# A hand-written order of 300 steps, written anew, with two filler matmuls fewer

## The chip, the cores and the metric

The kernel runs on one core of a Trainium2 chip. A core has five engines that run their own instruction queues and wait for each other through semaphores: TensorE (PE; its weight loads are shown apart as PEld), VectorE (DVE), ScalarE (ACT), GpSimd (POOL) and SyncE (SP), which here issues nearly all DMAs. The metric is the device time of one execution in microseconds.

## The reference

The input x (2048 tokens of 448) is normalized over its columns. The output is x plus two branches of the normalized xn: a linear attention and a feed-forward block.

```python
def _A_ref(x, wqkv, w_phi, wo):
    qkv = (x @ wqkv)...                                  # 16 heads of 28
    pq = jnp.einsum("bhsd,hdf->bhsf", q, w_phi)
    pk = jnp.einsum("bhsd,hdf->bhsf", k, w_phi)
    phi_q = concatenate([softmax(pq), softmax(-pq)])
    phi_k = concatenate([softmax(pk), softmax(-pk)])
    kv = einsum("bhsf,bhsd->bhfd", phi_k, v); z = phi_k summed over s
    num = einsum("bhqf,bhfd->bhqd", phi_q, kv)
    den = einsum("bhqf,bhf->bhq", phi_q, z)[..., None] + 1e-6
    return (num / den) @ wo
def _B_ref(x, w1, b1, w2):
    h = x @ w1 + b1                                      # 1792 columns
    return (h * tanh(softplus(h))) @ w2
xn = _layernorm(x)
return x + _A_ref(xn, ...) + _B_ref(xn, ...)
```

## The kernel before

Tokens are taken in 16 tiles t of 128, two tiles to a unit u. Everything is written as small named steps, and one string, `ORDER`, lists the roughly 300 steps in the order in which they are recorded (`run_order`). Recording a step appends its instructions to the queues of the engines that it uses, so this one list sets the order on every engine at once; `Program.resolve` then adds the semaphore waits that the data need. PSUM banks are handed out in the order of recording too: `take2` gives the pair of banks that was used longest ago, so a step waits for whatever last read those banks. Engines run in order: an instruction that waits holds up all behind it on its queue, and on SP it holds up every later DMA.

The names. `lx..`, `lkm`, `lkt`, `lvm`, `l1..`, `l2`, `lo`, `lb` load x, the k weights (three chunks of 128 rows, then the tail of 64 rows twice), v's, W1 (three chunks `l1m0` to `l1m2` and tails `l1t`), W2, Wo and the bias; `lqT0` to `lqT3` load wqkv's q columns with a DMA transpose (L285). `z18` is 18 filler matmuls on a constant (L376), which nobody reads. `st6d` is the statistics of tile 6 on VectorE (`a`: on ScalarE), `rs`/`xn` the normalization of a unit (L464 to L492; `p`: on POOL, `d`: on VectorE), and `xt` the transposition of xn into xnT, where contraction runs over partitions: by TensorE and copies (`b`, `a`, `d`; L500), or by one DMA transpose from SP (`m`; L512). `wtk` transposes the k weights on TensorE (L552) and `wmk`, `wmq` multiply phi into the k and q weights (L576), so that pk and pq come from xn directly.

`k2F` and `k2H` are the two parts of unit 2's matmuls for k, `q2F` and `q2H` for q, `v2F` and `v2H` for v, all of them at L430: the contraction of 448 is three whole chunks of 128 rows (F, six matmuls for the two tiles) and a half chunk of 64 rows (H, two matmuls on two halves of the array). F and H may stand in either order, with other steps between; after the second, ScalarE or VectorE empties the two banks: for k and q with two exps each (L614, L675), for v with a copy (L505 or L507). `e3` is the DMA transpose of tile 3's exps of q (L683), again from SP. `kn2.0` sums exps of k per head on VectorE (L622, L624) and scales them on POOL (L626). `f1.2F`/`f1.2H` are the two parts of the FFN's first product for the second half of the tokens and chunk 2 of 14 (L430), followed by ScalarE's Mish (L694). `kv0` to `kv7` (L643) sum phi_k with v, `kvz` brings that into a masked form and transposes it by DMA (L661). `nd5` is the numerator and denominator of tile 5 (L717) and its seven VectorE operations (L732 to L743), `ot` the transposition of the result by DMA (L752), `g5` the FFN's second product for tile 5 (L818), `wo2F`/`wo2H` the output projection of unit 2 (L834), then VectorE adds the residual (L783) and `sto` stores. On POOL, `pi` makes the identity matrix that TensorE's transposes read and the small constant in the normalization's root, `pm`, `pk` masks, `pw`, `pp`, `pv` fills, `bd` the block-diagonal phi.

The tiles keep the names of their buffers in the trace: exps of q lie in `actT` or `Eq`, exps of k in `actT`, xn in four buffers, and the transposed attention results take the places of `Wkv`, `WqT` and `Wpk`.

Of the kernel before, what the change touches and what calls it, by code (L numbers as in the profile page):

```python
# [144 lines left out]


ORDER = """
lx3s lx1s lkms lpa lkts lvms lx2s lqT1 lqT2 st6d table z18 pi st7a pp rs3t st2d st3d pw pm pv lqT0 lqT3 lx6s xn3d rs1a
xn1d wtk0b xt3b wtk1b bd xt1b wmk0a st5d v3Ha st4d qd lx0s v3Fa lx4s wmk1a rs2p xn2p v1Fd wmq1d wmq0a k1F st14d k1H
st15d rs7p v1Hd xn7p xt2m q3H q1H st8d st9d st11d st1d q3F rs4p pk xn4d q1F k3F st10d l1m0s k3H rs5p k2H st12d st0d  # L150
rs0p st13d xn5d q2H lbs q2F k2F xt7m e3 rs6p xt4m e2 xn6p e7 v2Fa v7Fa k7F xt5m v2Hd xn0p v7Hd k7H kn7.0 kn2.0 l1m2s
q4H q4F k4F kn1.0 kn2.1 v4Fa v4Ha k4H e4 k5H xt6m v5Ha kn1.1 kn7.1 v5Fa k5F q6F xt0m kn3.0 k6F k6H v6Hd e6 e5 q6H q5H
l1ts v6Fd q5F l1m1s v0Fd e8 k0F kn5.1 b1 kn6.0 k0H kn3.1 kn4.1 v0Ha f1.2H f1.3H e12 e11 f1.2F f1.3F f0.2F e9 f1.5F e10
e13 f0.2H kn5.0 f1.5H q0H q7H kn4.0 kn0.1 kn6.1 q7F ep kn0.0 f1.0F f0.5F q0F f0.1F f0.1H f1.0H f0.5H kv3 kv1 kv6 kv2
kv4 e15 e0 kv5 kv7 kv0 e14 f0.8H f1.8H f0.8F kvz f0.13F f1.8F f0.7F f0.13H nd3 f1.6H f0.7H e1 f1.6F f0.12F nd1 f0.12H
nd2 f0.3H f0.3F ot1m l2s los f0.11F f0.6F f0.6H f0.11H nd6 f1.1H f1.1F f0.10F f1.11H nd7 f0.9H f0.10H ot3m f0.9F
f1.11F f1.12F f0.4H nd11 f1.9H f0.4F f1.9F f1.4F f1.4H f0.0H f1.12H nd0 ot0m wob f0.0F f1.10F f1.7F f1.13H nd10 f1.7H
f1.10H f1.13F g1 nd4 nd5 ot2m ot5m nd12 wo0H g0 wo1F g3 wo0F g10 nd13 wo1H wo5H nd14 g11 wo5F sto0 ot6m g2 g4 nd15 nd9
wo2H nd8 g5 g13 g14 wo3F ot7m wo7F wo2F g7 g9 g6 g12 wo7H wo3H ot4m sto1 stt14 wo6H wo4H wo4F sto3 wo6F g8 sto5 sto2
sto4 g15 sto6 stt15  # L160
"""


# [806 lines left out]
```

## Time and profile before

| | us |
|---|---|
| median of 3 runs (153.37 to 154.47) | 154.28 |
| the profiled execution | 153.66 |
| its span on the core | 151.8 |
| TensorE busy in the span | 148.0 |

The granted TensorE clock is 1.00. In the views of the profile times count from the start of the span. A row of the timeline gives start, busy time, engine, line, operation and shape, and `xN` where N instructions of one line were merged; in brackets stands how long the engine sat idle before it and what released it. "SPq" rows are DMA issues on SP: their time is that of the issue, not of the transfer. The rows of DMA issues give the size and the median time from issue to landing. Matmuls are pipelined and their ends are modelled, so that their starts are compared, not their busy times.

### The profile page before, as it was taken

The page shows a single profiled execution, that of the slowest core. Times are in us where ns is not written, and L with a number is a line of the kernel's source. Part 1 is how long each engine was busy: PE and PEld are TensorE (multiplying, and loading weights), DVE is VectorE, ACT ScalarE, POOL GpSimd, SP SyncE. Part 2 cuts the span into 40 slices and gives each one's busy share as a digit, 9 for nine tenths or more (in the row PEclk, how much of TensorE's full clock was granted, in tenths as well). Part 3 has the DMA queues.
Part 4 walks back from the last instruction along what each step waited for, and adds up shares of the span by engine and source line. Part 5 has one row for each costly group of instructions (what it writes and reads, how often), then busy time and mean ns, then how long its engine had stood idle before and what let it go on. Part 6 is the DMA issues. An engine that isn't in the chain of part 4 may idle for free.

```text
span 151.8 us, 2910 instructions
## 1 busy us (share of the span) xinstructions
PE 148.0 (97%) x1187; PEld 73.1 (48%) x1187; DVE 100.1 (66%) x224; ACT 72.5 (48%) x87; POOL 45.0 (30%) x66
## 2 busy tenths in 40 slices
PE   7999999999999999999999999999999999999993
PEld 2565454444344466444444444555554655554452
DVE  0977997998799603079986477597896894300631
ACT  3886997897898997585664767000000000000000
POOL 7315888999999960000000000000000000000000
DMA  4997789999996095700099703005230031300234
GB/s 136 294 135 292 181 153 182 223 211 151 224 235 126 0 107 109 138 0 0 15 225 347 173 4 60 0 4 107 77 60 0 4 60 32 89 4 0 95 117 151
DMA packets 39994, 17.17 MB, mean 113 GB/s; under 512 B 33965, under 2 KB 39213, under 8 KB 39981
## 3 DMA queue, kind: packets, MB, share of 16 engines
q1 hardware_dynamic: 39372, 16.87, 50.6%
q8 instruction: 9, 0.15, 0.4%
q10 hardware_dynamic: 608, 0.12, 0.4%
q14 instruction: 5, 0.03, 0.1%
HBM read 7.02 MB, written 1.84 MB: 58 GB/s over the span
## 4 chain that ended last, share of the span: by engine, by line
PE 92%; DMA 2%; SPq 2%; DVE 1%; issue 0%
PE PS L430 46%; PE PS L818 28%; PE PS L834 7%; PE PS L376 4%; PE PS L717 3%; DMA xnT<-xn 2%; PE PS L643 2%; PE PS L576 1%; SPq L683 1%; DVE v_all L507 1%; PE PS L500 1%; PE PS L552 1%; SPq L277 1%; DVE x_all L783 0%; SPq L512 0%
## 5 line engine op out<-in xcount | busy, mean ns | idle before, releaser
L430 PE MATMUL PS<-xnT,W 128*128 128x512 bf16 (+1 forms) x224 | 46.0, 380 | 0.3 <-issue 0.3
L818 PE MATMUL PS<-W,actT 128*128 128x448 bf16 (+1 forms) x224 | 43.5, 351 | 0.0
L694 ACT ACTIVATE actT<-PS,b1T 128x1024 bf16<-128x1024 f32 x28 | 30.0, 1112 | 14.1 <-PE PS L430 14.0
L818 PEld LDWEIGHTS PS<-W,actT 128*128 128x128 bf16 x224 | 21.7, 98 | 20.0 <-DVE v_all L738 0.2
L430 PEld LDWEIGHTS PS<-xnT,W 128*128 128x128 bf16 (+1 forms) x224 | 17.7, 97 | 24.9 <-issue 6.1
L626 POOL TENSOR_TENSOR actT<-actT,rSk 128x896 bf16<-128x896 bf16 x16 | 26.6, 1697 | 0.6 <-DVE rSk L624 0.6
L783 DVE TENSOR_TENSOR x_all<-PS,x_all 128x448 bf16<-128x448 f32 (+1 forms) x16 | 9.3, 615 | 16.4 <-PE PS L834 13.1
L622 DVE TENSOR_REDUCE Sk<-actT 128x32 f32<-128x896 bf16 x16 | 16.6, 1040 | 0.0
L614 ACT ACTIVATE actT<-PS 128x896 bf16<-128x896 f32 x16 | 14.0, 938 | 3.1 <-PE PS L430 3.1
L430 PE MATMUL PS<-Wkv,xnT 128*128 128x448 bf16 (+1 forms) x64 | 12.8, 353 | 0.0
L430 PE MATMUL PS<-Wpk,xnT 128*128 128x448 bf16 (+1 forms) x64 | 12.7, 353 | 0.0
L430 PE MATMUL PS<-Wpq,xnT 128*128 128x448 bf16 (+1 forms) x64 | 12.3, 352 | 0.2 <-DMA xnT<-xn 0.2
L743 DVE TENSOR_TENSOR xn<-v_all,rden 128x448 bf16<-128x448 f32 x16 | 10.0, 625 | 3.8 <-DMA Wkv<-xn 3.3
L732 DVE COPY Sq<-PS 128x16 f32<-128x16 f32 x32 | 4.0, 168 | 12.0 <-PE PS L717 12.0
L458 DVE BATCH_NORM_STATS2 stats<-x_all 128x6 f32<-128x448 bf16 x15 | 9.1, 604 | 3.7 <-DMA x_all<-in_A_x_dram 3.7
L740 DVE TENSOR_TENSOR v_all<-v_all 128x464 f32<-128x464 f32 x16 | 10.3, 643 | 0.6
L736 DVE TENSOR_TENSOR v_all<-PS,Sq 128x464 f32<-128x464 f32 x16 | 10.3, 641 | 0.5
L738 DVE TENSOR_TENSOR v_all<-PS,Sq 128x464 f32<-128x464 f32 x16 | 10.1, 630 | 0.0
L810 POOL COPY WoB<-Wo 64x64 bf16<-64x64 bf16 x1 | 0.2, 234 | 30.4 <-DMA Wo<-in_A_wo_dram 30.4
L675 ACT ACTIVATE actT<-PS 128x896 bf16<-128x896 f32 x10 | 8.7, 944 | 0.0
L430 PEld LDWEIGHTS PS<-Wpq,xnT 128*128 128x128 bf16 (+1 forms) x64 | 5.1, 97 | 6.4 <-issue 1.5
L430 PEld LDWEIGHTS PS<-Wpk,xnT 128*128 128x128 bf16 (+1 forms) x64 | 5.3, 97 | 5.5 <-issue 1.1
(84 smaller groups left out, 126.0 us busy)
## 6 DMA issues: line engine op xcount, KB each, us to landing
W<-in_B_w_dram SPq DMA_DIRECT2D x1, 1568.0 KB, 7.4
out_dram<-x_all SPq DMA_DIRECT2D x7, 224.0 KB, 2.2
W<-in_B_w_dram SPq DMA_DIRECT2D x3, 448.0 KB, 3.9
x_all<-in_A_x_dram SPq DMA_DIRECT2D x4, 224.0 KB, 3.4
x_all<-in_A_x_dram SPq DMA_DIRECT2D x2, 448.0 KB, 4.3
Wkv<-in_A_wqkv_dram SPq DMA_DIRECT2D x2, 336.0 KB, 4.6
Wo<-in_A_wo_dram SPq DMA_DIRECT2D x2, 336.0 KB, 8.0
W<-in_B_w_dram SPq DMA_DIRECT2D x2, 224.0 KB, 4.1
```

Of the source, the lines that this page charges most:

```text
L430: ins = e.matmul(o, lhs(c, k), rhs(c, k), start=first and c in (0, 3), stop=not first and c in (2, 3))
L614: op("ACT", lambda e, s=s: e.activation(E_of(u)[:, s, :, :], two(b, D), ACT.Exp, scale=1.0 if s == 0 else -1.0), r=[pb(b), pb(b + 1)], w=[ ...
L622: op("DVE", lambda e: e.tensor_reduce(Sk[u][:, s, :], Eh(), AX.X, ALU.add), r=[("E", u, s)], w=[("Sk", u, s)], tag=f"Sk{u}.{s}")
L626: op("POOL", lambda e: e.tensor_tensor(Eh(), Eh(), ap_on(rSk[u][:, s, 0:1], [[1, 2 * H], [0, DH]]), ALU.mult), r=[("E", u, s), ("rSk", u, ...
L694: op("ACT", lambda e: e.activation(actT[:, fc, q * 1024:(q + 1) * 1024], bank(b, 2), ACT.Mish, bias=b1T[:, fc:fc + 1]), r=[("b1T",), pb(b) ...
L736: op("DVE", lambda e: e.tensor_tensor(tv(t1[i]), num(0), sx(1), ALU.mult), r=[pb(b), pb(b + 1), ("Sq", i, 1)], w=[("t1", i)], tag=f"ta{t}")
L738: op("DVE", lambda e: e.tensor_tensor(tv(t2), num(1), sx(0), ALU.mult), r=[pb(b), pb(b + 1), ("Sq", i, 0)], w=[("t2",)], tag=f"tb{t}")
L740: op("DVE", lambda e: e.tensor_tensor(t1[i], t1[i], t2, ALU.add), r=[("t1", i), ("t2",)], w=[("t1", i)], tag=f"tc{t}")
L743: op("DVE", lambda e: e.tensor_tensor(o_sb[(t // 2) % 2][:, t % 2, :].rearrange("p (h d) -> p h d", d=DH), t1[i][:, :, 0:DH], ap_on(rden[i ...
L783: op("DVE", lambda e: e.tensor_tensor(x_all[:, t, 0:n], bank(b)[:, 0:n], x_all[:, t, 0:n], ALU.add), r=[pb(b), ("x", t)], w=[("out", t)], ...
L818: ins = e.matmul(bank(b)[:, 0:width(t)], actT[:, fc, tok(t)], W2[:, fc, 0:width(t)], start=first and fc == 0, stop=last and fc == FC - 1)
L834: ins = e.matmul(bank(b)[:, 0:n], oT_of(u)[lo:hi, cc * P:(cc + 1) * P], Wo[lo:hi, cc, 0:n], start=first and c in (0, 3), stop=last and c i ...
```

## The change

Only the string `ORDER` changes; the steps themselves are the same, with these exceptions: `z16` stands for `z18`; some steps run in another form or on another engine (statistics of tile 5 and the roots for units 2 and 6 on ScalarE, xn of unit 6 on VectorE and not on POOL, unit 1's transposed xn copied by VectorE alone, copies of v and of the weights dealt out anew). The first line before and after:

```diff
-lx3s lx1s lkms lpa lkts lvms lx2s lqT1 lqT2 st6d table z18 pi st7a pp rs3t st2d st3d pw pm pv lqT0 lqT3 lx6s xn3d rs1a
+pm pw lx3s pp pk lx1s lkms lkts st6d lpa table pi st7a st2d st3d rs3t xn3d lvms rs1a z16 xn1d bd wtk0b wtk1b lx2s xt3b
```

At three places the queues now read as follows. First TensorE from its first instruction to the q weights: fillers (L376), the transposes of the k weights (`ident,Wkv`) and of xn of units 3 and 1, phi times the k weights (`Wbd,Eq`), the first v and k parts, phi times the q weights (`Wbd,WqT`). Before:

```order
L376 MATMUL PS<-const-bfloat16-1.0 128x512 x18
L552 MATMUL PS<-ident,Wkv 112x128 x8
L500 MATMUL PS<-ident,xn 128x128 x7
L552 MATMUL PS<-ident,Wkv 112x128 x8
L500 MATMUL PS<-ident,xn 128x128 x7
L576 MATMUL PS<-Wbd,Eq 128x112 x8
L430 MATMUL PS<-Wkv,xnT 128x448 x8
L576 MATMUL PS<-Wbd,Eq 128x112 x8
L430 MATMUL PS<-Wkv,xnT 128x448 x6
L576 MATMUL PS<-Wbd,WqT 128x112 x16
```

And now:

```order
L376 MATMUL PS<-const-bfloat16-1.0 128x512 x16
L552 MATMUL PS<-ident,Wkv 112x128 x16
L500 MATMUL PS<-ident,xn 128x128 x14
L576 MATMUL PS<-Wbd,Eq 128x112 x16
L430 MATMUL PS<-Wkv,xnT 128x448 x8
L430 MATMUL PS<-Wpk,xnT 128x448 x2
L430 MATMUL PS<-Wkv,xnT 128x448 x8
L576 MATMUL PS<-Wbd,WqT 128x112 x16
```

The second transposes of the k weights, which read the tails too, stand directly behind the first, both xn transposes behind them, and unit 3's half chunk for k and unit 1's for v now come ahead of the q weights.

Second, SP from the q weights' transposing loads (L285) to the first transposed xn (L512). Before:

```order
L285 DMA_TRANSPOSE WqT<-in_A_wqkv_dram 128x448 x4
L270 DMA x_all<-in_A_x_dram 128x1792
L270 DMA x_all<-in_A_x_dram 128x896
L270 DMA x_all<-in_A_x_dram 128x1792
L512 DMA_TRANSPOSE xnT<-xn2 128x7x128
L277 DMA W1<-in_B_w1_dram 128x1792
L302 DMA b1_rows<-in_B_b1_dram 14x128
L512 DMA_TRANSPOSE xnT<-xn3 128x7x128
```

And now:

```order
L285 DMA_TRANSPOSE WqT<-in_A_wqkv_dram 128x448 x2
L270 DMA x_all<-in_A_x_dram 128x896
L285 DMA_TRANSPOSE WqT<-in_A_wqkv_dram 128x448 x2
L270 DMA x_all<-in_A_x_dram 128x1792 x2
L302 DMA b1_rows<-in_B_b1_dram 14x128
L512 DMA_TRANSPOSE xnT<-xn2 128x7x128
L281 DMA W1<-in_B_w1_dram 64x1792 x2
L512 DMA_TRANSPOSE xnT<-xn3 128x7x128
```

The x load of tiles 0 and 1 moved ahead of the last two transposing loads, and so ahead of the load of tiles 12 to 15 (the first of those of 128x1792); W1's tails took the place of its first chunk.

Third, SP from there on, up to W1's last piece: transposed xn (buffers `xn0`, `xn1`, `xn2` and again `xn0` are units 4, 5, 6 and 0), transposed exps of q (L683, two to a unit) and W1. Before:

```order
L683 DMA_TRANSPOSE EqT<-actT 128x8x128
L512 DMA_TRANSPOSE xnT<-xn0 128x7x128
L683 DMA_TRANSPOSE EqT<-actT 128x8x128
L683 DMA_TRANSPOSE EqT<-Eq0 128x8x128
L512 DMA_TRANSPOSE xnT<-xn1 128x7x128
L277 DMA W1<-in_B_w1_dram 128x1792
L683 DMA_TRANSPOSE EqT<-actT 128x8x128
L512 DMA_TRANSPOSE xnT<-xn2 128x7x128
L512 DMA_TRANSPOSE xnT<-xn0 128x7x128
L683 DMA_TRANSPOSE EqT<-Eq0 128x8x128
L683 DMA_TRANSPOSE EqT<-actT 128x8x128
L281 DMA W1<-in_B_w1_dram 64x1792 x2
```

(one more piece of W1, 128x1792, follows). And now:

```order
L683 DMA_TRANSPOSE EqT<-actT 128x8x128
L512 DMA_TRANSPOSE xnT<-xn0 128x7x128
L683 DMA_TRANSPOSE EqT<-actT 128x8x128
L512 DMA_TRANSPOSE xnT<-xn1 128x7x128
L512 DMA_TRANSPOSE xnT<-xn2 128x7x128
L277 DMA W1<-in_B_w1_dram 128x1792
L512 DMA_TRANSPOSE xnT<-xn0 128x7x128
L683 DMA_TRANSPOSE EqT<-actT 128x8x128 x2
L277 DMA W1<-in_B_w1_dram 128x1792
L683 DMA_TRANSPOSE EqT<-Eq0 128x8x128
L277 DMA W1<-in_B_w1_dram 128x1792
```

Units 5 and 6 stand further ahead, with fewer transposes of q between, and the three chunks of W1 are spread among what follows.

On POOL, all of `pm`, `pw`, `pp` and `pk` now stand ahead of `pi`, and xn of unit 6 is gone from it. On TensorE the units' parts of k, q and v are dealt out in another order behind the q weights, from `k3F` on; the FFN parts, the nd, g and wo steps too, in another order with the same kinds.

More of the change, by code (lines that the diff above doesn't have):

```diff
@@ L147 @@
 ORDER = """
-lx3s lx1s lkms lpa lkts lvms lx2s lqT1 lqT2 st6d table z18 pi st7a pp rs3t st2d st3d pw pm pv lqT0 lqT3 lx6s xn3d rs1a
[L149 to L157, printed above, removed]
@@ L158 @@
-f1.10H f1.13F g1 nd4 nd5 ot2m ot5m nd12 wo0H g0 wo1F g3 wo0F g10 nd13 wo1H wo5H nd14 g11 wo5F sto0 ot6m g2 g4 nd15 nd9
-wo2H nd8 g5 g13 g14 wo3F ot7m wo7F wo2F g7 g9 g6 g12 wo7H wo3H ot4m sto1 stt14 wo6H wo4H wo4F sto3 wo6F g8 sto5 sto2
-sto4 g15 sto6 stt15
+pm pw lx3s pp pk lx1s lkms lkts st6d lpa table pi st7a st2d st3d rs3t xn3d lvms rs1a z16 xn1d bd wtk0b wtk1b lx2s xt3b
+pv xt1d wmk0b wmk1a lqT0 st5a st4d lqT2 lx0s lqT3 lqT1 v3Fa v3Hd qd lx6s rs2a k3H lx4s v1Ha lbs st0d xn2p v1Fd st14d
+wmq1a wmq0a xt2m st15d k3F st13d k1F l1ts q3H rs7p k1H xn7p q1H st8d st9d q1F st11d st10d rs4p rs5p xt7m e3 xn4d q3F
@@ new lines @@
+q2F st12d v2Fd q2H xn5d v2Hd st1d rs6a k2H xt4m k2F xn6d v7Fa e2 xt5m xt6m k7F v7Ha k7H l1m2s rs0p k4H xn0p v4Ha v4Fa
+k4F kn3.1 kn7.1 k5F k5H k6H v5Ha xt0m k6F kn7.0 v5Fa e4 q4F kn2.1 kn2.0 e5 l1m1s v6Fa b1 q4H v6Hd k0H e7 kn3.0 q5H q5F
+l1m0s k0F kn4.1 kn1.0 q6F e6 kn6.0 v0Fd v0Hd q6H kn6.1 f1.2H f1.5H kn0.0 kn4.0 kn5.1 f1.2F e11 e9 e10 f1.5F e13 e8
+f1.3F f0.2F f0.2H ep q7H kn0.1 e12 q0H f1.3H kn5.0 q7F q0F f1.0F kn1.1 f0.1F f0.8F f1.0H f0.1H kv3 kv4 kv6 kv2 kv7 kv5
+kv0 e0 e15 kv1 f0.8H f0.5H kvz e1 f1.12H f0.5F f1.12F f1.9F f1.7F f1.7H f1.8H f1.9H nd2 f1.8F f0.13F f0.13H e14 f0.0H
@@ L161 @@
+f1.1H nd3 f0.0F f0.3F f1.1F ot1m f1.13F f0.3H l2s los nd6 f0.7H f1.13H f0.7F f1.10F f0.10F nd0 f0.10H f1.10H f1.4H
+f1.4F f0.6F nd1 ot0m f0.9H f0.6H nd7 f0.9F f1.6F f0.11F f0.11H nd5 f0.12H ot3m f1.6H f0.12F wob f0.4F f0.4H nd4 ot2m
+f1.11H nd13 f1.11F g5 g1 wo0H nd10 nd12 wo2H wo2F g4 g0 ot6m wo0F nd9 nd11 wo1H g3 g2 wo1F sto2 ot5m wo3F nd15 nd14
+wo3H nd8 ot7m g7 g8 g6 g14 g12 g10 g13 wo7F g9 wo5F sto0 wo6F wo7H wo5H ot4m wo6H wo4H wo4F sto3 sto4 stt14 g11 g15
+sto5 sto6 sto1 stt15
 """
```

## The prediction

> **What bounds the kernel now.** I read the page's head first, then the chain that ended last, then the engine views in order of time at each place where the chain leaves TensorE.
>
> The page's span and its row of busy time:
>
> ```profile
> span 151.8 us, 2910 instructions
> PE 148.0 (97%) x1187; PEld 73.1 (48%) x1187; DVE 100.1 (66%) x224; ACT 72.5 (48%) x87; POOL 45.0 (30%) x66
> ```
>
> TensorE has work in 97% of the span, no other engine in more than two thirds, and the change keeps every matmul but two fillers. So the time can move only by TensorE's waits, by the start and by the tail. Its rows in order of time, cut to the four places where it starts late and to one run of matmuls that starts on time beside each (start, busy time, operation, count):
>
> ```profile
> 6.28 0.63 PE L552 MATMUL PS<-ident,Wkv 128*112 128x128 bf16 x8
> 6.90 0.56 PE L500 MATMUL PS<-ident,xn 128*128 128x128 bf16 x7
> 7.30 0.61 PE L552 MATMUL PS<-ident,Wkv 128*112 128x128 bf16 x8
> 7.75 0.55 PE L500 MATMUL PS<-ident,xn 128*128 128x128 bf16 x7
> ...
> 10.47 1.30 PE L430 MATMUL PS<-Wkv,xnT 128*128 128x448 bf16 x6
> 11.80 0.96 PE L576 MATMUL PS<-Wbd,WqT 112*128 112x112 bf16 x16
> 12.60 1.59 PE L430 MATMUL PS<-Wpk,xnT 128*128 128x448 bf16 x8
> ...
> 31.05 1.30 PE L430 MATMUL PS<-Wpk,xnT 128*128 128x448 bf16 x6
> 32.56 1.29 PE L430 MATMUL PS<-Wpq,xnT 128*128 128x448 bf16 x6 [0.22 <-DMA xnT<-xn]
> 33.70 1.59 PE L430 MATMUL PS<-Wpk,xnT 128*128 128x448 bf16 x8
> 35.13 0.35 PE L430 MATMUL PS<-Wkv,xnT 64*128 64x448 bf16 x2
> ...
> 40.55 0.36 PE L430 MATMUL PS<-Wpk,xnT 64*128 64x448 bf16 x2
> 40.74 0.35 PE L430 MATMUL PS<-Wkv,xnT 64*128 64x448 bf16 x2
> 41.42 0.93 PE L430 MATMUL PS<-xnT,W 64*128 64x512 bf16 x5 [0.32 <-issue]
> ```
>
> Starts are compared, since the ends overlap. A whole-chunk part (six matmuls, F) takes 33.70 - 32.56 = 1.14 us, a half-chunk part (two, H) 40.74 - 40.55 = 0.19. An F and an H take 35.13 - 33.70 = 1.43, so a change from one kind to the other costs 0.10. The waits of before, beyond these: the transposes of unit 3's xn start 6.90 - 6.28 - 0.45 = 0.17 late (0.45 is 7.75 - 7.30), the q weights' matmuls 11.80 - 10.47 - 1.14 = 0.19, `q6F` 32.56 - 31.05 - 1.14 = 0.37, the first FFN part `f1.2H` 41.42 - 40.74 - 0.19 = 0.49. Together **1.22 us**, all that an order can win in the body.
>
> Two of the four are SP's. The chain gives for `q6F` the transfer of unit 6's transposed input, which it waits for:
>
> ```profile
> 28.70 3.73 DMA xnT<-xn
> ```
>
> It lands at 32.43, behind a row of q transposes in SP's queue. `f1.2H` needs all of W1, whose last piece was issued at 36.56 and took
>
> ```profile
> W<-in_B_w_dram SPq DMA_DIRECT2D x1, 448.0 KB, 4.8
> ```
>
> so it landed at 41.3.
>
> **The change, part by part.** *The two fillers.* Loads of weights for the fillers, the first weights' load of the real work, and the loads that it needs (issue, and time to landing; the row of L281 gives the last of the two tails' starts):
>
> ```profile
> 3.35 0.15 PEld L376 LDWEIGHTS PS<-const-bfloat16-1.0 128*128 128x128 bf16 x1 [0.28 <-issue]
> 3.78 2.15 PEld L376 LDWEIGHTS PS<-const-bfloat16-1.0 128*128 128x128 bf16 x10 [0.28 <-issue]
> 6.25 0.51 PEld L552 LDWEIGHTS PS<-ident,Wkv 128*112 128x112 bf16 x8 [0.33 <-issue]
> ```
> ```profile
> 1.72 0.43 SPq L273 DMA_DIRECT2D Wkv<-in_A_wqkv_dram  x1
> ```
> ```profile
> Wkv<-in_A_wqkv_dram SPq DMA_DIRECT2D x1, 336.0 KB, 4.4
> ```
> ```profile
> L281 SPq DMA_DIRECT2D Wkv<-in_A_wqkv_dram x2: 557/574/590, 2.2 to 2.8; - x2
> ```
> ```profile
> Wkv<-in_A_wqkv_dram SPq DMA_DIRECT2D x2, 112.0 KB, 4.3
> ```
>
> A filler costs 0.43 us until 3.78 and 2.15 / 10 = 0.215 after, so two are 0.43. But the k weights land at 1.72 + 4.4 = 6.12, and the transposes start 0.1 later, at 6.25: fillers and load end together. SP's first seven issues are unchanged. **I count the fillers at nothing**: TensorE idles 0.4 us there instead. POOL now makes all its masks and pads ahead of the identity that the transposes read. They stood in two stretches (start and end, length, then busy time and count of TensorE, its loads, VectorE, ScalarE and POOL):
>
> ```profile
> 0.80:3.46 2.66, 2.62 (x7) 0.98 (x8) 0.00 (x0) 1.28 (x1) 2.22 (x11) 1.00 0.57 160
> 19.32:21.37 2.05, 2.05 (x13) 1.04 (x12) 2.02 (x7) 2.05 (x4) 1.71 (x7) 1.00 0.77 147
> ```
>
> Back to back, 2.66 + 2.05 from 0.80, the identity is there at 5.5; its cover, to 6.25, is 0.7 us, and a delay past that would delay all.
>
> *The second weight transposes come one step earlier.* They need the k weights' tails, which land at 2.8 + 4.3 = 7.1. Ready at 6.28 + 0.45 = 6.73, they start at 7.16: **0.43 us lost**, and the 0.17 is gone, since xn is then long done. Queued behind them on TensorE are xn's transposes, and behind those ACT's and DVE's copies.
>
> *The q weights.* SP's issues of the transposed q weights, the next x load, landings, and the DVE copy that waits for the last of them:
>
> ```profile
> 4.58 5.12 SPq L285 DMA_TRANSPOSE WqT<-in_A_wqkv_dram  x4
> 9.75 0.59 SPq L270 DMA_DIRECT2D x_all<-in_A_x_dram  x1
> ```
> ```profile
> x_all<-in_A_x_dram SPq DMA_DIRECT2D x1, 448.0 KB, 3.9
> WqT<-in_A_wqkv_dram SPq DMA_TRANSPOSE x1, 3.1
> ```
> ```profile
> 11.52 0.23 DVE L289 COPY WqT<-WqT 128x256 bf16<-128x256 bf16 x1 [1.06 <-DMA WqT<-in_A_wqkv_dram]
> ```
>
> One x load (about 0.47) now stands between them, so the last starts at 4.58 + 3 x 1.28 + 0.47 = 8.9, lands at 12.0, and the copy lets TensorE go at 12.3. TensorE itself gets there by 7.16 and what lies between: the 4.5 us from 7.30 to 11.80, less the 0.19, plus 0.40 for xn's transposes, two H and a change (0.48): 12.3. The old wait of 0.19 becomes about 0.05.
>
> *Feeding the transposed x.* For unit 7, POOL's normalization and SP's issues after it:
>
> ```profile
> 16.67 1.73 POOL L487 TENSOR_SCALAR xn<-x_all,rstd,shift 128x448 bf16<-128x448 bf16 x3 [0.37 <-DVE shift L480]
> ```
> ```profile
> 18.42 1.24 SPq L512 DMA_TRANSPOSE xnT<-xn  x1
> 19.71 1.31 SPq L683 DMA_TRANSPOSE EqT<-actT  x1
> ```
> ```profile
> xnT<-xn SPq DMA_TRANSPOSE x6, 3.3
> ```
>
> The x load for units 6 and 7 goes out 0.47 later, so it lands at 10.2 + 3.9 = 14.1 and not 13.65, and what hangs on it (statistics, POOL's normalization to 18.4, the issue at 18.42) slides with it: unit 7's transpose is issued at 18.9 and lands at 22.2. Then SP issues one transpose each 1.29 to 1.36: e3, unit 4, e2, unit 5 (24.2), unit 6 (25.5), with two e's and a load of W1 fewer ahead of unit 6 than before. They land 3.3 (the page's median) to 3.7 (the chain's row) later: unit 5 at 27.5 to 28.0, unit 6 at 28.8 to 29.3. TensorE asks for unit 7 after 12.3 + 0.8 (the q weights) + 7 F + 6 H + 4 changes = 22.6, for unit 5 another 4 F, 4 H and 2 changes later, 28.1, and for unit 6 at 29.5. So each is there, by 0.1 to 0.6 us: **the 0.37 goes**, and what is late next is unit 5, with almost no slack.
>
> *W1.* Its tails now go out ahead of unit 7, and its last piece, behind unit 0, e4, e5 and e7, at 33.8; by the 4.8 us it is there at 38.6. `f1.2H` comes at 28.1 + 9 F + 9 H + five changes and the bias (0.1) = 40.6. **The 0.49 goes**, with 2 us to spare.
>
> *The rest.* Changes between F or g parts and H or nd parts are 39 for 38, 0.1 us. ScalarE's exps keep their number; TensorE runs behind them with 0.3 to 0.6 us in hand around unit 4. In the FFN and attention part TensorE had no wait in before; there each nd is still fed by one DVE chain and I find none that grows. The tail ends on the same g15, last columns and store.
>
> **Sum:** -1.22 + 0.43 + 0.05 + 0.1 = -0.64; the four places are read to some 0.05 each, so -0.65. The profiled execution took 153.66 us (span 151.8, 1.8 us around it) and would take 153.0. It lies 0.6 below the median of the runs shown, 154.28, and I carry the difference to that: **153.6 us**.
>
> **Rivals.**
> *The start gives more.* The fillers' pace turned from 0.43 to 0.215 at 3.78. Were that three fillers later in another execution, 18 fillers would end 0.65 later, at 6.9, past the load, and 16 at 6.5: the change then wins up to 0.43. The 0.6 us between the profile and the median leaves room for it; against it, the profile shows one execution. Also the tails may land earlier than asked. Time: 152.7 to 153.2. The Trainium skill (TensorE: Matmul & The Clock Gate, Part 1: The HAM clock gate) states that the window which frees the clock runs freely, so the number of slow first matmuls varies from run to run; by that rule this rival would hold in some runs, and the one trace here can't show it.
> *The feed is late, and the kernel slower.* One mechanism: x's load for units 6 and 7 starts the chain of transposes, and SP's queue passes each delay on. Should that load take 4.8 us (as W1's piece of the same size did), not 3.9, units 7, 5 and 6 land 0.9 later: unit 7 at 23.1 stops TensorE 0.6, unit 5 at 28.4 to 28.9 another 0 to 0.4, and at 1.43 us an issue it loses 0.5 more. With 0.6 to 1.5 us lost the time is 154.2 to 155.1; it decides from 0.65, where the gain is used up. For it: four transposes and another load stand ahead of that load on the DMA rings. Against: 3.9 was taken with the same transposes ahead.
> *Nothing is won.* If SP's wins at `q6F` and `f1.2H` only move to waits on ScalarE's exps, which hold TensorE's banks, 0.86 comes back and the time is 154.4; the 0.3 to 0.6 us in hand speak against it.
> *A wait far behind,* where before shows none: q7's and q0's exps need q transposes at the end of SP's row, the products with v need POOL's last scaling. With the late feed this would be 155.8 and more.
>
> **How the numbers follow.** Forecast 0.50 (153.2 to 154.0); the start gives more 0.17; the feed is late 0.15; nothing won 0.08; a wait far behind 0.10. One in ten below and one in ten above leave 152.6 to 155.6. One per cent, 1.5 us, is about what a measurement of this kernel can tell from no change. Faster by that is below 152.7: the better part of the first rival, 0.12. Slower is above 155.8: the last case and the end of the late feed, 0.13. Within: 0.75.
>
> **What would show it.** Right: fillers end at 5.8 and the first transposes still start near 6.25; the second weight transposes at 7.1 to 7.2; no wait over 0.1 at `q6F` and `f1.2H`; the last g15 0.6 to 0.7 earlier. Wrong: TensorE waiting for xnT between 22 and 30 us (late feed), for an exp of k4, k5 or q4 (nothing won), or for EqT or POOL between 44 and 57 us.

## The result, and the profile after

Both kernels were run in turn on one chip, 22 executions of each. The changed kernel's median is **153.31 us** (153.02 to 154.09), that of the kernel before 154.16 (153.35 to 154.96); the ratio is **0.9946, with a 95% interval of 0.9931 to 0.9962**. Timed once more beside later experiments, the ratio was 0.9932 (0.9904 to 0.9961). So 0.85 us are gone, where the prediction had 0.65 under the profiled execution and 153.6 us for the median.

The span and the busy times on the page of the changed kernel:

```profile
span 151.5 us, 2903 instructions
PE 147.3 (97%) x1185; PEld 73.2 (48%) x1185; DVE 101.9 (67%) x224; ACT 74.1 (49%) x96; POOL 41.4 (27%) x59
```

The profiled execution took 153.24 us. The span shrank by only 0.3, but this execution's first weights came late. What TensorE waited for, in all, times, longest (the view of waits, TensorE alone), before:

```profile
PE PS L376 <- PEq L955: 0.8, 1, 0.8
PE PS L430 <- issue: 0.3, 1, 0.3
PE PS L430 <- DMA xnT<-xn: 0.2, 1, 0.2
```

and after:

```profile
PE PS L552 <- DMA Wkv<-in_A_wqkv_dram: 0.9, 2, 0.6
PE PS L376 <- PEq L955: 0.8, 1, 0.8
```

The two rows at L430, the prediction's `f1.2H` and `q6F`, are gone, and no wait at L430 took their place. The new row is the weights' load, twice: the main part, then the tails. The timeline of TensorE after, at the places that the prediction named (start, busy time, line and tiles, count, idle time before):

```profile
6.78 0.62 PE L552 MATMUL PS<-ident,Wkv 128*112 128x128 bf16 x8 [0.63 <-DMA Wkv<-in_A_wqkv_dram]
7.63 0.65 PE L552 MATMUL PS<-ident,Wkv 128*112 128x128 bf16 x8 [0.23 <-DMA Wkv<-in_A_wqkv_dram]
8.12 0.94 PE L500 MATMUL PS<-ident,xn 128*128 128x128 bf16 x14
...
12.74 0.95 PE L576 MATMUL PS<-Wbd,WqT 112*128 112x112 bf16 x16
...
23.03 1.30 PE L430 MATMUL PS<-Wkv,xnT 128*128 128x448 bf16 x6
...
27.41 2.92 PE L430 MATMUL PS<-Wpk,xnT 128*128 128x448 bf16 x16
30.16 0.35 PE L430 MATMUL PS<-Wkv,xnT 64*128 64x448 bf16 x2
...
40.91 0.35 PE L430 MATMUL PS<-Wpq,xnT 64*128 64x448 bf16 x2
41.10 5.23 PE L430 MATMUL PS<-xnT,W 64*128 64x512 bf16 x25
...
148.35 0.25 PE L797 MATMUL PS<-Wo,Wpk 128*128 128x64 bf16 x3
```

By starts: the second weight transposes 7.63 - 6.78 - 0.45 = 0.40 late, and from there on nothing: the q weights at 12.74, unit 7 at 23.03, units 4 to 6 without a gap from 25.6 to 30.5, the first FFN part 41.10 - 40.91 = 0.19 behind the half chunk ahead of it, its bare length. Before, the same last columns (L797) stood here:

```profile
148.69 0.25 PE L797 MATMUL PS<-Wo,Wpk 128*128 128x64 bf16 x3
```

From the first weight transposes to these columns TensorE needed 148.69 - 6.28 = 142.41 us before and 148.35 - 6.78 = **141.57** after: 0.84 less, which fits the 0.85 of the medians. The 0.3 of the spans is this less the 0.50 by which the weights came later in the profiled execution after; that part varies from one execution to the next (below). The profiled execution before, with its early weights, lies 0.50 under its kernel's median of 154.16, the one after only 0.07 under its own. The chain of work that ended last says the same: it leaves the tails of the k weights and then stays on TensorE for good.

```profile
2.79 4.80 DMA Wkv<-in_A_wqkv_dram
7.63 0.65 PE PS L552 x8
8.28 0.78 PE PS L500 x14
9.06 0.79 PE PS L576 x16
9.85 3.05 PE PS L430 x18
```

On SP, the transposes of units 7, then 5 and 6 (the merged row), W1's last piece and the transpose of q behind it:

```profile
19.07 1.23 SPq L512 DMA_TRANSPOSE xnT<-xn  x1
...
24.42 2.67 SPq L512 DMA_TRANSPOSE xnT<-xn  x2
...
34.00 0.58 SPq L277 DMA_DIRECT2D W<-in_B_w_dram  x1
34.62 1.69 SPq L683 DMA_TRANSPOSE EqT<-Eq  x1
```

Their landings, by the DMA events of the trace: unit 7 at 22.02, asked for at 23.03; unit 5 at 28.13, asked for at 28.55; unit 6 at 29.04, asked for at 29.98. W1's last piece, as the DMA view shows it for the window of its issue (KB, us from issue to landing):

```profile
W<-in_B_w_dram SPq DMA_DIRECT2D x1, 448.0 KB, 6.5
```

It landed at 40.45, 0.65 ahead of the first FFN part.

### The profile page after: what moved, and what is told of

Read it like the earlier page. It is cut to its first block, busy times and chain, and to the rows that moved or that the text cites. A ratio compares the mean times of both kernels' runs of the same rounds, so it can differ in the third digit from the quotient of the medians.

```text
span 151.5 us, 2903 instructions
## 1 busy us (share of the span) xinstructions
PE 147.3 (97%) x1185; PEld 73.2 (48%) x1185; DVE 101.9 (67%) x224; ACT 74.1 (49%) x96; POOL 41.4 (27%) x59
## 4 chain that ended last, share of the span: by engine, by line
PE 93%; DMA 3%; SPq 1%; DVE 0%; issue 0%
PE PS L430 51%; PE PS L818 28%; PE PS L834 7%; DMA Wkv<-in_A_wqkv_dram 3%; PE PS L717 3%; PE PS L643 2%; PE PS L576 1%; SPq L270 1%; PE PS L500 1%; PE PS L552 0%; DVE x_all L783 0%; SPq L281 0%; SPq L273 0%; DVE x_all L804 0%; PE PS L688 0%
## 5 line engine op out<-in xcount | busy, mean ns | idle before, releaser
L430 PE MATMUL PS<-xnT,W 128*128 128x512 bf16 (+1 forms) x224 | 45.8, 379 | 0.0
L818 PE MATMUL PS<-W,actT 128*128 128x448 bf16 (+1 forms) x224 | 43.0, 351 | 0.0
L430 PEld LDWEIGHTS PS<-xnT,W 128*128 128x128 bf16 (+1 forms) x224 | 17.8, 97 | 23.8 <-issue 5.1
L614 ACT ACTIVATE actT<-PS 128x896 bf16<-128x896 f32 x16 | 13.5, 953 | 0.0
L430 PE MATMUL PS<-Wkv,xnT 128*128 128x448 bf16 (+1 forms) x64 | 13.0, 353 | 0.0
L430 PE MATMUL PS<-Wpq,xnT 128*128 128x448 bf16 (+1 forms) x64 | 12.5, 353 | 0.0
L430 PE MATMUL PS<-Wpk,xnT 128*128 128x448 bf16 (+1 forms) x64 | 12.4, 352 | 0.0
L458 DVE BATCH_NORM_STATS2 stats<-x_all 128x6 f32<-128x448 bf16 x14 | 8.5, 607 | 3.8 <-DMA x_all<-in_A_x_dram 3.8
L675 ACT ACTIVATE actT<-PS 128x896 bf16<-128x896 f32 x10 | 8.7, 932 | 0.9 <-PE PS L430 0.8
L430 PEld LDWEIGHTS PS<-Wpq,xnT 128*128 128x128 bf16 (+1 forms) x64 | 5.2, 97 | 6.0 <-issue 1.9
L430 PEld LDWEIGHTS PS<-Wkv,xnT 128*128 128x128 bf16 (+1 forms) x64 | 5.3, 97 | 5.9 <-issue 1.9
```

The lines of the kernel that those rows point to most:

```text
L430: ins = e.matmul(o, lhs(c, k), rhs(c, k), start=first and c in (0, 3), stop=not first and c in (2, 3))
L614: op("ACT", lambda e, s=s: e.activation(E_of(u)[:, s, :, :], two(b, D), ACT.Exp, scale=1.0 if s == 0 else -1.0), r=[pb(b), pb(b + 1)], w=[ ...
L818: ins = e.matmul(bank(b)[:, 0:width(t)], actT[:, fc, tok(t)], W2[:, fc, 0:width(t)], start=first and fc == 0, stop=last and fc == FC - 1)
```

## Experiments

Two theories stood against each other at first. The prediction's: the gain is the two waits on SP's transfers (`q6F`, `f1.2H`), less the tails' wait at the start, and the fillers are worth nothing. The first rival's: fewer fillers let the start begin sooner. All kernels were timed in five rounds beside the kernel before, each group on one chip. "Body" is the time from the first weight transposes to the last columns at L797, in the profiled execution; it leaves out how late the first weights came.

### The fillers alone

The kernel before, with `z16` for `z18` and nothing else.

> The kernel before with 16 fillers in place of 18, nothing else. Theory (the k weights' load, not the fillers, sets the start of the first transposes): no change, 0.0 us, within 0.15; fillers end 0.43 earlier and TensorE idles that long before 6.2 to 6.8. Rival (the fillers end last in most executions, so that the change's gain is theirs): 0.3 to 0.45 us faster.

Measured: 154.31 us against 154.20; ratio 1.0019 (0.9990 to 1.0048). Two fillers fewer give nothing, and a gain over 0.15 us is outside the interval. In the profiled execution the slow pace of the fillers lasted long. Its weight loads for the last filler, and for the first transposes:

```profile
6.77 0.11 PEld L376 LDWEIGHTS PS<-const-bfloat16-1.0 128*128 128x128 bf16 x1 [0.28 <-issue]
7.18 0.51 PEld L552 LDWEIGHTS PS<-ident,Wkv 128*112 128x112 bf16 x8 [0.30 <-issue]
```

Here 14 of the 16 ran at the slow pace, 0.43 us apart, up to 6.8 us, and the last ended at 7.2. But the weights landed only at 7.08, and the transposes started at 7.22, 0.14 behind them: as far behind as in the executions whose fillers had long ended (0.13 to 0.14). So load and fillers ended together here, and the fillers held nothing up. The rival's mechanism does exist, though. In the run below that moves W1's tails alone, with 18 fillers, 11 were slow; the weights landed at 6.36, and the first transposes started only at 7.11, 0.75 behind them. Its last weight loads for fillers, and those for the transposes:

```profile
5.79 0.98 PEld L376 LDWEIGHTS PS<-const-bfloat16-1.0 128*128 128x128 bf16 x5 [0.16 <-issue]
6.89 0.68 PEld L552 LDWEIGHTS PS<-ident,Wkv 128*112 128x112 bf16 x8
```

In the 13 profiled executions of this study with 16 or 18 fillers the slow pace lasted for 7 to 14 of them; in all 14 profiled executions the main k weights landed between 5.94 and 7.08 us (issued at 1.72 in each). The Trainium skill (TensorE: Matmul & The Clock Gate, Part 1: The HAM clock gate) says that the window which frees the clock runs freely, so that the same kernel shows different counts of slow matmuls; the 7 to 14 agree. In nine of the 13, load and last filler ended within half a microsecond of each other, and in only three did the transposes start more than 0.14 behind the weights (0.20, 0.35 and 0.75), so that fewer fillers can win little.

### Far fewer fillers

The changed kernel with eight.

```diff
-... rs1a z16 xn1d bd wtk0b ...
+... rs1a z8 xn1d bd wtk0b ...
```

> The changed kernel with 8 fillers in place of 16. The fillers then end near 4.3 us and TensorE idles until the k weights land at 6.2 to 7.1. Theory (the fillers' number doesn't set the start, but their running keeps the pace fast): the transposes still start at 6.2 to 7.1, but where the pace had not turned by 4.3 us, or falls back in the idle 2 us, the first real matmuls run at half pace: 0.3 to 1.5 us slower than the changed kernel. Rival (the pace doesn't matter that early, since loads and copies pace TensorE until 12 us): no change.

Measured: 154.67 us (153.42 to 156.14) against 154.44; ratio 1.0022 (0.9991 to 1.0053), so about 1.2 us slower than the changed kernel, and wider spread. TensorE's rows in the profiled execution:

```profile
6.08 1.92 PE L552 MATMUL PS<-ident,Wkv 128*112 128x128 bf16 x16 [1.67 <-DMA Wkv<-in_A_wqkv_dram]
7.79 1.45 PE L500 MATMUL PS<-ident,xn 128*128 128x128 bf16 x14
9.08 0.95 PE L576 MATMUL PS<-Wbd,Eq 112*128 112x112 bf16 x16
```

The 16 weight transposes and most of xn's start 0.107 us apart instead of 0.055: the slow pace lasts into the real work, up to 8.86 us. From the first weight transposes to the products with phi it took 9.08 - 6.08 = 3.00 us, against 8.90 - 6.78 = 2.12 after. This is what the fillers are for. The profiled execution was the fastest of its twelve (153.42 us): its weights landed at 5.94, 0.70 earlier than in the profiled execution after, which makes up for most of the 0.88 lost here. Between 16 and 18 the difference can't be measured, between 8 and 16 it is about 1.2 us by the ratios.

### Each of SP's two waits alone, in the kernel before

W1's tails out of their place behind `q5H`, ahead of unit 7's transpose:

```diff
-... q2H lbs q2F k2F xt7m e3 ...
-l1ts v6Fd q5F l1m1s ...
+... q2H lbs l1ts q2F k2F xt7m e3 ...
+v6Fd q5F l1m1s ...
```

> The kernel before with W1's two tail loads issued right behind the bias, ahead of unit 7's transpose, where SP idled 1.4 us; nothing else moves. Theory (the wait of 0.49 us at f1.2H is SP's late issue of W1): W1's last piece is issued about 2 us earlier and the wait goes: 0.4 to 0.5 us faster. Rival (the wait only turns into one for ScalarE's exp of unit 5's q, which frees the banks): 0.0 to 0.2 us faster, with f1.2H waiting for exq5.

Measured: 154.15 against 154.20; ratio 0.9994 (0.9970 to 1.0018). A miss: `f1.2H` no longer waits, but unit 7 does. The waits of TensorE for transposed xn, now two (unit 7, and `q6F` as before):

```profile
PE PS L430 <- DMA xnT<-xn: 0.8, 2, 0.6
```

By starts, `v7F` is 0.72 late. Unit 7's transpose landed at 23.32, 4.3 us after its issue, where it took 3.03 before; the two tails were issued just ahead of it.

The other wait alone: `e7` behind unit 6's transpose.

```diff
-... e2 xn6p e7 v2Fa v7Fa ... e4 k5H xt6m v5Ha ...
+... e2 xn6p v2Fa v7Fa ... e4 k5H xt6m e7 v5Ha ...
```

> The kernel before with tile 7's transposed exps of q issued behind unit 6's transposed xn in place of ahead of unit 5's; nothing else moves. Theory (the wait of 0.37 us at q6F is the place of unit 6's transpose in SP's row): units 5 and 6 are issued 1.35 us earlier, q6F starts without a wait, 0.35 us faster, if no wait behind it grows: f1.2H's own wait of 0.49 stays or grows by the 0.37 that TensorE comes earlier, since W1's last piece lands when it did. In that case alone it gives nothing: 0.0. So this run tells whether the two waits are in series behind one queue.

Measured: 154.71 against 154.20; ratio 1.0050 (1.0025 to 1.0075). A miss again, and slower, by some 0.8 us by the ratio. The wait at `q6F` is gone, but everything that comes behind on SP is later, and W1's last piece with it: issued at 37.76 (before: 36.56), landed at 42.78.

```profile
40.71 0.35 PE L430 MATMUL PS<-Wkv,xnT 64*128 64x448 bf16 x2
42.87 3.30 PE L430 MATMUL PS<-xnT,W 64*128 64x512 bf16 x16 [1.80 <-DMA W<-in_B_w_dram]
```

`f1.2H` is 42.87 - 40.71 - 0.19 = 1.97 late instead of 0.49. The two waits that the prediction added up are tied to each other through the same queue.

### Both together, in two forms

Both moves in the kernel before, tails ahead of unit 7's transpose:

> The kernel before with both moves on SP: W1's tails early and tile 7's transpose behind unit 6's. Theory (SP's row alone makes both waits): 0.75 to 0.9 us faster, as much as the whole change, though every step on TensorE, ScalarE and VectorE stands as before. Rival (the new order on the computing engines is needed): less than 0.4 us faster.

Measured: 153.98 against 154.20; ratio 0.9989 (0.9969 to 1.0009). Both old waits are gone, and one stands in for them:

```profile
21.05 1.30 PE L430 MATMUL PS<-Wkv,xnT 128*128 128x448 bf16 x6
23.53 1.30 PE L430 MATMUL PS<-Wkv,xnT 128*128 128x448 bf16 x6 [1.18 <-DMA xnT<-xn]
```

Unit 7's `v7F` is 23.53 - 21.05 - 1.14 = 1.34 late: its transpose, issued at 18.60, took 4.8 us. That is more than the two old waits together (0.86), and the body is 142.51 us, no shorter than before. Was that only the tails' place? Directly behind unit 7's transpose instead:

```diff
-... q2H lbs l1ts q2F k2F xt7m e3 ...
+... q2H lbs q2F k2F xt7m l1ts e3 ...
```

> The kernel before with both moves on SP (`e7` behind unit 6's transpose, W1's tails out of the place behind `e5`), but the tails not ahead of unit 7's transpose as in the run that made v7F wait 1.35 us: directly behind it. Everything on TensorE stays as before the change, 18 fillers and POOL's order too. Theory 1 (the gain is SP's order alone, and the 1.35 was the tails' data ahead of unit 7's): unit 7 lands by 22.1, v7F waits 0.2 us at most, q6F and f1.2H not at all, what may be late next is unit 5 with 0 to 0.4; the time is 0.5 to 0.85 us below before, a ratio of 0.9945 to 0.997. Theory 2 (with before's order on TensorE the queue has no place for the tails): another transposed xn, of unit 7, 4 or 5, stops TensorE by 0.6 us or more, and the ratio is 0.998 to 1.003.

Measured: 154.05 against 154.78; ratio 0.9985 (0.9958 to 1.0012). Unit 7 now lands in time (21.75), and unit 4, behind the tails, does not:

```profile
25.55 0.35 PE L430 MATMUL PS<-Wpk,xnT 64*128 64x448 bf16 x2
26.46 1.61 PE L430 MATMUL PS<-Wpq,xnT 64*128 64x448 bf16 x8 [0.55 <-DMA xnT<-xn]
```

It is 26.46 - 25.55 - 0.19 = 0.72 late, for a landing at 26.32. Theory 2 of that run holds: with before's W1 chunk early on SP, before's order on TensorE and the tails added, some transposed xn is late with the tails in either of the two places.

The change does two things more. It does not add the tails to the early queue, it exchanges them for a chunk of W1 of the same total size (448 KB), which now goes out last; and TensorE asks for unit 7 later: 23.03 - 6.78 = 16.25 us behind the first weight transposes, where the run with both moves was ready for it at 22.19 - 6.53 = 15.66.

No run makes one of these without the other, but the traces say where the landings moved. Unit 7's transpose took 3.03 us before, with a chunk of W1 as the one W1 load shortly ahead of it, 2.95 after, with the tails as that load, and 4.8 with both; it landed at 22.02 after the change and at 23.39 in the first run here, while TensorE asked at 23.03 and 22.19. Unit 4's landed at 24.73 and, in the second run, at 26.32, while TensorE asked at 25.79 and 25.74. So for unit 4 nearly the whole difference is SP's queue, and for unit 7 the larger part.

### The same two moves, undone in the changed kernel

`e7` back ahead of unit 5's transpose:

```diff
-... v7Fa e2 xt5m xt6m ... k0H e7 kn3.0 ...
+... v7Fa e2 e7 xt5m xt6m ... k0H kn3.0 ...
```

> The changed kernel with tile 7's transposed exps of q issued ahead of unit 5's transposed xn, as in the kernel before. Theory (SP's row feeds TensorE just in time): unit 5 lands at 29.4 in place of 28.1, TensorE asks at 28.55, so k5F starts 0.9 to 1.0 us late; the time is 0.8 to 1.0 above the changed kernel's, about 1.001 of before. Rival (slack hides it): 0.0 to 0.2 above the changed kernel.

Measured: 154.62 against 154.44; ratio 1.0025 (0.9995 to 1.0054), so 1.2 us above the changed kernel. Unit 5 is late, as expected:

```profile
27.20 1.30 PE L430 MATMUL PS<-Wpk,xnT 128*128 128x448 bf16 x6
29.55 1.78 PE L430 MATMUL PS<-Wpk,xnT 128*128 128x448 bf16 x10 [1.05 <-DMA xnT<-xn]
```

29.55 - 27.20 - 1.14 = 1.21, for one transpose of 1.3 us on SP. That is the slack that the prediction gave unit 5, almost none.

W1's tails back behind `e5`:

```diff
-... k1F l1ts q3H rs7p ...
-... e4 q4F kn2.1 kn2.0 e5 l1m1s ...
+... k1F q3H rs7p ...
+... e4 q4F kn2.1 kn2.0 e5 l1ts l1m1s ...
```

> The changed kernel with W1's two tails issued behind e5, ahead of the last two chunks of W1, in place of ahead of unit 7's transpose. Theory: W1's last piece is issued 1.3 us later and lands at 41.7 or later, TensorE asks at 41.1, so f1.2H waits 0.6 to 1.3 us and the time rises by that, to 0.999 to 1.003 of before; unit 7's transpose, now without loads ahead of it, lands a little earlier, which gives nothing. Rival (the DMA rings are shared, so that only the order of landing matters and W1 is there in time): no change from the changed kernel.

Measured: 154.17 against 154.44; ratio 1.0003 (0.9975 to 1.0032), above the changed kernel by 0.9 us, though the intervals leave some 0.4 to 1.4. In the profiled execution `f1.2H` is 0.30 late (W1's last piece landed at 41.61):

```profile
41.21 0.35 PE L430 MATMUL PS<-Wpq,xnT 64*128 64x448 bf16 x2
41.70 2.66 PE L430 MATMUL PS<-xnT,W 64*128 64x512 bf16 x13
```

The 0.30 is shown; the rest of the 0.9 lies outside this row and is left open (in that execution 14 slow fillers, ending at 7.2, held the start up too).

### Winning back the tails' wait

The changed kernel loses 0.40 us behind the tails. The transposes of unit 3's xn, put between the two weight transposes as they stood before, would fill it if xn were there.

```diff
-... bd wtk0b wtk1b lx2s xt3b
+... bd wtk0b xt3b wtk1b lx2s
```

> The changed kernel with unit 3's xn transposes put back between the first and the second transposes of the k weights. Theory (the one wait left in the changed kernel, 0.40 us, is for the k weights' tails, and other work is ready there): the wait shrinks to 0.0 to 0.05, the time is 0.35 to 0.4 us under the changed kernel's, about 0.992 of before. Rival (what the tails hold up is hidden anyway behind the q weights at 12.3 to 12.7, which wait for their own load): 0.0 to 0.1 under the changed kernel.

Measured: 153.41 against 154.44; ratio 0.9957 (0.9938 to 0.9975), no better than the change. A miss: xn was not there.

```profile
6.43 0.62 PE L552 MATMUL PS<-ident,Wkv 128*112 128x128 bf16 x8 [0.43 <-POOL Wbd L535]
7.49 0.56 PE L500 MATMUL PS<-ident,xn 128*128 128x128 bf16 x7 [0.44 <-DVE xn L492]
```

(The first row's releaser is only the last event that the view found; the weights had landed at 6.29.) The transposes of xn start 7.49 - 6.43 - 0.45 = 0.61 late, waiting for VectorE. Its six instructions at L492 in the kernel before, from the timeline and from the line's own view (count, ns min/median/max):

```profile
5.91 1.74 DVE L492 TENSOR_SCALAR xn<-x_all,mv,rstd 128x448 bf16<-128x448 bf16 x6
```
```profile
L492 DVE TENSOR_SCALAR xn<-x_all,mv,rstd x6: 299/371/395, 5.9 to 7.3; 128x448 bf16<-128x448 bf16 x2, 128x64 bf16<-128x64 bf16 x2, 128x384 bf16<-128x384 bf16 x2
```

and after, with what POOL did meanwhile:

```profile
5.98 2.25 DVE L492 TENSOR_SCALAR xn<-x_all,mv,rstd 128x448 bf16<-128x448 bf16 x6
```
```profile
L492 DVE TENSOR_SCALAR xn<-x_all,mv,rstd x6: 283/368/957, 6.0 to 7.9; 128x448 bf16<-128x448 bf16 x2, 128x64 bf16<-128x64 bf16 x2, 128x384 bf16<-128x384 bf16 x2
```
```profile
5.26 1.08 POOL L535 TENSOR_TENSOR Wbd<-Wraw,mask 112x224 bf16<-112x224 bf16 x2
6.28 0.53 POOL L341 MEMSET v_all<- 128x256 uint32 x1
```

The first of the six took 957 ns, longer by 0.56 us than any of them before, and ended at 6.94, just behind POOL's fill (6.81). Before, POOL had finished both by 5.1. So a new theory: POOL's new order at the start holds VectorE up. It was tested with POOL's masks `pk` put off and the fill of v_all ahead of phi (two words of `ORDER` moved), beside the changed kernel itself, and then with xn's transposes between the weights' as well.

```diff
-pm pw lx3s pp pk lx1s lkms lkts st6d lpa table pi st7a ...
-pv xt1d wmk0b ...
-... rs4p rs5p xt7m ...
+pm pw lx3s pp lx1s lkms lkts st6d lpa table pi pv st7a ...
+xt1d wmk0b ...
+... rs4p rs5p pk xt7m ...
```

> The changed kernel once more, on the same chip as the next two. Both theories: a ratio to before of 0.992 to 0.997, the first normalization on VectorE (tensor_scalar to xn) 0.90 to 1.05 us long, with its end at most 0.2 us behind the end of POOL's fill of v_all, and the second transposes of the k weights 0.3 to 0.5 us late behind the load of the tails.

> The changed kernel with POOL's work at the start in another order: the masks and fill of `pk` later, near 22 us, and the fill of v_all ahead of the block-diagonal phi, so that POOL is done by some 5.0 us, before VectorE starts the normalization at 6.0. Theory 1 (POOL's instructions beside it held the first normalization up): it takes 0.36 to 0.40 us, the six together 1.7 to 1.8 instead of 2.25, unit 3's xn is there by 6.9. Theory 2 (the first normalization is slow for another reason, such as its scalars that ScalarE has just written): it stays at 0.9 to 1.05. Time: both theories the same as the changed kernel, within 0.002 of its ratio, since TensorE waits for the tails of the k weights at that place, not for xn.

> As the run before, and on TensorE the transposes of unit 3's xn stand between the two transposes of the k weights, as they do before the change. Theory 1: xn of unit 3 is there by 6.9, so its transposes start behind the first weights' without a wait over 0.1 us and fill the time in which the tails land; the 0.4 us that the changed kernel loses there shrink to 0.1 or less, and the time is 0.3 to 0.4 us under the changed kernel, a ratio to before of 0.990 to 0.994. Theory 2: the transposes wait 0.5 to 0.6 us for xn as they did without POOL's new order, and the ratio stays within 0.002 of the changed kernel's.

Measured, in this order: 153.41, 153.56 and 153.40 against 154.48; ratios 0.9932 (0.9904 to 0.9961), 0.9943 (0.9915 to 0.9971), 0.9935 (0.9907 to 0.9963). In the changed kernel the longest of the six took 1044 ns again; with POOL's work earlier:

```profile
L492 DVE TENSOR_SCALAR xn<-x_all,mv,rstd x6: 294/370/390, 6.0 to 7.3; 128x448 bf16<-128x448 bf16 x2, 128x64 bf16<-128x64 bf16 x2, 128x384 bf16<-128x384 bf16 x2
```
```profile
5.95 1.74 DVE L492 TENSOR_SCALAR xn<-x_all,mv,rstd 128x448 bf16<-128x448 bf16 x6
```

Theory 1 holds: it was POOL. In all six profiled executions with the changed kernel's order on POOL, the first of the six instructions took 953 to 1071 ns and ended at 6.93 to 6.95, whenever it started (5.86 to 5.98); in the eight other executions it took 365 or 366. And with xn there, its transposes follow the first weights' without a wait:

```profile
7.12 0.62 PE L552 MATMUL PS<-ident,Wkv 128*112 128x128 bf16 x8
7.58 0.55 PE L500 MATMUL PS<-ident,xn 128*128 128x128 bf16 x7
7.97 0.61 PE L552 MATMUL PS<-ident,Wkv 128*112 128x128 bf16 x8
8.41 0.55 PE L500 MATMUL PS<-ident,xn 128*128 128x128 bf16 x7
```

The body falls to 141.36 us, 0.21 under the changed kernel's 141.57 (141.55 in its second profile), and not the 0.3 to 0.4 expected: the second products of phi with the k weights are now 0.18 late. Bodies of the same order differ by as much: in the kernel before with 16 fillers it was 142.65, against 142.41 with 18. The medians of the three do not differ by what these intervals can tell. No version here was shown to beat the changed kernel.

## Why the prediction was right

The median fell by 0.85 us, to 153.31; the forecast was 153.6, and under one per cent.

- **The sum.** Of -1.22 + 0.43 + 0.05 + 0.1, the first two terms came as worked out: the four waits went, and the tails cost 0.40 for the 0.43. The two small ones, 0.15 together, did not show: the q weights were there (the last transposing load landed at 12.03, as predicted; TensorE came at 12.74), and -1.22 + 0.40 = -0.82 is the body's -0.84 already. This is the term that was mis-sized. The account also leaves nothing for the other steps that stand in a new order, form or engine. The 0.05 for the q weights had no fair test: the copy behind that load ended at 12.63, and TensorE came 0.45 later than worked out.
- **The fillers at nothing.** Right for the time. Its reason, that load and fillers end together, is one execution's: they part by up to 0.8 us either way, and in the two profiled executions of the changed kernel the fillers ended 0.7 to 0.8 us ahead of the load. The first rival's mechanism was seen in three of the 14 profiled executions, in which 11 to 14 fillers were slow and the transposes started 0.06, 0.21 and 0.61 later behind the weights than the usual 0.14; it was worth nothing that the medians show.
- **POOL's identity at 5.5**, with cover to 6.25: its last instruction ended at 5.3, and nothing waited for it. But the same step overlooked what stands behind it on POOL, phi and v_all. "xn is then long done" was **wrong**: unit 3's xn was ready at about 7.4, some 0.6 later than before (its transposes could start at 7.49 in the run above, at 6.90 before). The tails, which came at 7.58, hid that. It cost nothing in the two profiled executions of the change, but that is luck: in the run with `e7` early, whose start is the same, the weights landed at 6.14, and TensorE waited 0.22 among the transposes of xn. It also cost the first attempt at the tails' wait.
- **The feed.** Unit 7 was predicted to land at 22.2, unit 5 at 27.5 to 28.0, unit 6 at 28.8 to 29.3; they landed at 22.02, 28.13 (just behind its range) and 29.04, and TensorE asked 0.45 later than worked out because its start was later by as much. With a start as early as before's, unit 5 would have been close to late; one more transpose ahead of it cost 1.2 us.
- **W1.** Issued at 34.0 (predicted 33.8), but it took 6.45 us and not 4.8: "2 us to spare" were 0.65. In the second profiled execution of the changed kernel it took 4.19 us (issued at 35.57) and had 1.4 to spare.
- **The waits as a sum.** The prediction added the two SP waits as if each could be taken by itself. By themselves, one move won nothing and the other lost 0.5 us by the medians, and both together in the old order won nearly nothing, because each transfer that is moved makes another late. The sum came true since the new queue, which the prediction worked through landing by landing, also sends a chunk of W1 last.
- **Rivals.** The late feed did not come; the runs with one transpose more ahead of unit 5 and with both moves in the kernel before show its mechanism and its price, one wait of 0.7 to 1.35 us. Nothing held TensorE at ScalarE's exps, and nothing waited far behind.

## What to carry to other kernels

Waits behind one queue are not a list to be added up: ask, for each transfer moved, which one is late next, and expect to win when something that can wait leaves the queue. Whether a later consumer alone would do was not tried here. A gain counted from one profiled execution should leave out the start, where loads and TensorE's pace vary from one execution to the next by more than the change is worth. Where steps move between stretches, look also at what now runs beside an instruction, not only at what it waits for.

## What the runs showed of the hardware

- POOL's product and fill at the start held up a VectorE `tensor_scalar` from SBUF to SBUF (128x448, bf16) that began beside them: 953 to 1071 ns in six executions, 365 or 366 in the eight in which they had ended. Not every POOL instruction does so: near 20 to 25 us the same instruction took 364 to 391 ns beside POOL's masks (L353), scalings (L464) and products (L467), and VectorE's statistics took 0.59 to 0.63 us beside POOL in both kernels. The Trainium skill (GPSIMD Engine Reference, 8. Key points) states that POOL shares its SBUF interfaces with VectorE and contends with its instructions in a two-port mode or with two SBUF inputs. The first `tensor_scalar` is in keeping with that; the traces don't show its mode, nor why it was not held up beside the others.
- TensorE's slow pace at the start ended between 3.8 and 6.8 us of the span in runs of the same or nearly the same code, and at 8.9 where only eight fillers ran; matmuls were then at about half pace (0.43 for 0.215, 0.107 for 0.055). The granted clock of the profile doesn't show this: from 0.80 to 3.80 us it reads 1.00 before and after.
- One and the same load, of the main k weights, issued at 1.72 in every run, landed between 5.94 and 7.08.
- A 448 KB chunk of W1 took 3.6 to 5.3 us from issue to landing with more of W1 behind it, and 4.1 to 6.6 as W1's last piece (6.45 and 4.19 in the two profiled executions of the changed kernel). Unit 7's DMA transpose took 2.9 to 3.2 us, and 4.3 to 4.8 with W1's two tails issued directly ahead of it and a chunk of W1 ahead of these. What sets these durations was not tried.
